# A convolution and maxout kernel on one core: x loads with three buffers, output stores moved to SyncE's queue, DMA transposes placed ahead of loads

## The chip, the cores and the metric

The kernel runs on one core of a Trainium2 chip. The time is device microseconds from launch to end; what is compared is the median over several runs. Before the change it is 467.4 us (five runs: 466.04, 466.86, 467.4, 467.55, 468.59).

## The reference

Input x has 8 sequences of 4160 tokens with 192 channels. First comes a causal convolution of 7 taps along the sequence, whose weights are a softmax per head (8 heads of 24 channels). Then every token goes through a maxout layer: three products with 192x768 weights, the largest of the three, and a product with a 768x192 weight.

```python
w = exp(weight - max) / (sum + 1e-9)                        # 8 heads x 7 taps
y[b, s, h, :] = sum_k w[h, k] * x_pad[b, s + k, h, :]        # 6 zero rows ahead of each sequence
h = np.maximum(np.maximum(y @ w1, y @ w2), y @ w3)           # 33280 x 768
out = h @ w_out                                              # 33280 x 192
```

## The kernel before

**Blocks.** The 33280 tokens are cut into 65 blocks of 512. Blocks 0 to 3 ("dense") take one road through the convolution, all later ones another. Blocks from 5 are convolved in pairs and from 17 (QUADS) in fours: one convolution serves four blocks.

**Stages of a later block.** `load_x(t)` (L129) brings 512 tokens of x into an fp32 buffer `xf` by two (sometimes three, once eight) DMAs on SyncE's queue, SP. There are seven such buffers (XBUF, L116), used in turn; `get_x` (L118) clears the unused rows of a buffer once, with a memset on GpSimd (POOL). `cast_x(t)` (L169) turns xf into fp16 by two POOL instructions, and frees the buffer. `conv` multiplies with a banded matrix on TensorE (L326), `evac` (L367) copies the sums out of PSUM to `ys`, `turn(t)` (L378) sends them through DMA transposes (L388, on SP) into `yp`, channels on partitions, and `double(t)` (L391) copies each half of `yp` to the other half of the partitions, by POOL, for blocks 4 and 5 by two DMAs on SP. `l1(t, j)` (L460 on) makes the first layer in six parts (L473: products lp and lq on the two halves of TensorE's rows; ScalarE and VectorE make the maximum, L480, L481). `st2(t, upto)` makes the second layer (L530); `total` adds its two halves into an output tile `o` (L538, L539), and `store` (L558 on) sends it away.

**Dense blocks.** Blocks 0 to 3 are cast by `cast_dense` (L189, block 2 and 3 wholly on POOL, L198), convolved by `conv_dense` (L345), and their halves are crossed between partitions, for block 3 by `cross_dma` (L363), two DMAs `yd<-yd` on SP (L365, L366).

**The order.** It is written out by hand. Each engine, and SP, does its instructions in the order in which the program names them. `op(fn)` puts a call behind the matmuls that are queued so far, `meet()` lets all queued work be placed. Ahead of the main loop (L617 to L634) stand the casts of `wo`, loads of blocks 6 to 10 among the rest, and `cast_dense(2)` and `(3)`. The loop over t (L653 on) makes, in turn t, the first layer of block t and the second of block t-1; `convs_at` (L643) says which later block is convolved in that turn (t is `late` where there is one); `casts` (L646) and `loads` (L649) say up to which block has been cast and loaded by turn t, about 8 and 10 blocks on:

```python
loads = {t: min(NB - 1, max(10, casts.get(t + 1, 0) + 1)) for t in range(3, NB)}
...
        if t > 3:
            for v in range(loads[t - 1] + 1, loads[t] + 1):
                load_x(v)
...
        op(lambda t=t: store(t - 2, 0, 4, (nc.gpsimd if t < NB - 1 else nc.sync,)))
...
                if second:
                    turn(u)
```

So in a turn the loads stand first on SP, and the transposes, four in a row for four blocks (in turn u - 3), behind them. Stores are issued from POOL (L569), each behind a wait for VectorE's last sum of that block (L539).

Of the kernel before, what the change touches and what calls it, by code (L numbers as in the profile page):

```python
# [28 lines left out]
def kernel(  # L29
# [12 lines left out]
    nc = tc.nc  # L42
# [27 lines left out]
    NB = len(blocks)  # L70
# [15 lines left out]
    NDENSE = 4  # L86
# [31 lines left out]
    def get_x(t):  # L118

        if not 0 <= t < NB or t in xin:  # L120
            return
        if t < XBUF:
            xbuf.append(const.tile([P, NR, D], FP32, name=f"xf_{t}"))
        xf = xbuf[t % XBUF]
        if NDENSE <= t < NDENSE + XBUF:
            nc.gpsimd.memset(xf[TOK:HALF, 0 if t < XBUF else NQ:NR, :], 0.0)  # L126
        xin[t] = [xf, 0, ()]

    def load_x(t, eng=nc.sync):  # L129
        if not 0 <= t < NB:  # L130
            return
        get_x(t)
        xf = xin[t][0]
        if t < NDENSE:
            todo = [(0, c[3], c[1] * SEQ + c[2], i) for i, c in enumerate(chunks_of[t])]
        else:
            todo = [(HALF * (i // NR) + (0 if s else LAP), KR if s else TOK,
                     b * SEQ + s - (LAP if s else 0), i % NR) for i, (b, s) in enumerate(rows_of(t))]
        parts = []
        i, n = 0, len(todo)  # L140
        row = [c[2] for c in todo]
        while i < n:
            k = i
            while k + 1 < n and todo[k + 1][:2] == todo[i][:2] and row[k + 1] - row[k] == row[i + 1] - row[i]:
                k += 1
            step = row[i + 1] - row[i] if k > i else 0
            p0, rlen, _, q0 = todo[i]
            q1 = todo[k][3] + 1
            src = bass.AP(tensor=x.tensor, offset=row[i] * D,
                          ap=[[D, rlen], [step * D, q1 - q0], [1, D]])  # L150
            eng.dma_start(out=xf[p0:p0 + rlen, q0:q1, :], in_=src)  # L151
            if parts and parts[-1][0] == rlen:
                parts[-1] = (rlen, parts[-1][1], q1)
            else:
                parts.append((rlen, q0, q1))
            i = k + 1
        xin[t] = [xf, todo[0][0], parts]
# [4 lines left out]
        pairs[t] = (t - u, u, 2 if t < QUADS else 4)  # L162

    def place(t):
        return pairs[t]

    x16s, slots = {}, {}

# [18 lines left out]
    xz[2], xz[3] = xz[0], xz[1]  # L187

    def cast_dense(t, copies):  # L189
        xf, _, parts = xin[t]  # L190
        for v, copy in enumerate(copies):
            if copy is None:
                continue
            for s in range(CYC // 32):
                cut = GRP * (32 * s // GRP + 1)
                a, b = (32 * s, cut) if v == 0 else (cut, 32 * s + 32)
                for (rl, q0, q1) in parts:
                    copy(  # L198
                        out=xz[t][v][0:rl, q0:q1, :].rearrange("p q (k c) -> p q k c", c=CYC)[:, :, :, a:b],
                        in_=xf[0:rl, q0:q1, :].rearrange("p q (k c) -> p q k c", c=CYC)[:, :, :, a:b])  # L200
# [174 lines left out]
                 "p u r (h c) -> p h (u r) c", c=GRP),  # L375
             in_=G[i][:].rearrange("p h (n c) -> p h n c", c=GRP))

    def turn(t):  # L378


        nu = place(t)[2]
        for v in range(0, nu, 2):
            n = min(nu, 2)
            yp = ypp.tile([P, 2, 2, n, NC, P], FP16, tag="yp", name=f"yp_{t + v}")
            for u in range(n):
                dense[t + v + u] = yp
            for i in range(2):
                nc.sync.dma_start_transpose(out=yp[:, 0, i, :, :, :].rearrange("p u k n -> p (u k) n"),  # L388
                                            in_=slots[t][:, i, v:v + n, :, :].rearrange("p u r d -> p (u r d)"))

    def double(t, by_dma=False):  # L391

        if not NDENSE <= t < NB:
            return
        yp = dense[t]
        copy = nc.sync.dma_start if by_dma else nc.gpsimd.tensor_copy
        for i in range(2):
            copy(out=yp[HALF * i:HALF * (i + 1), 1, :, :, :, :].rearrange("p i u k n -> p (i u k n)"),  # L398
                 in_=yp[HALF * (1 - i):HALF * (2 - i), 0, :, :, :, :].rearrange("p i u k n -> p (i u k n)"))
# [35 lines left out]
    def op(fn):  # L435
        ops.append((tuple(put), fn))
# [178 lines left out]
    l1(0, 4)  # L615
    meet()
    nc.gpsimd.tensor_copy(out=wo[:], in_=wos[:])  # L617
    for t in range(6, 9):
        load_x(t)
    l1(0, 5, WW)  # L620
    meet()
    make_m(0)
    make_m(1)
    cast_dense(2, (nc.gpsimd.tensor_copy, nc.gpsimd.tensor_copy))
    load_x(9)
    l1(1, 4)
    meet()
    st2(0, (5, 5))
    meet()
    conv_dense(2, (nc.scalar.copy, nc.vector.tensor_copy, nc.scalar.copy))  # L630
    cast_dense(3, (nc.gpsimd.tensor_copy, nc.gpsimd.tensor_copy))
    load_x(10)
    cast_x(4)
    cross(2)  # L634
    l1(1, 5)
# [10 lines left out]
    casts = {4: 9}  # L646
    for t in range(5, NB):
        casts[t] = min(NB - 1, casts[t - 1] + (2 if t in (6, 9, 12) else 1))
    loads = {t: min(NB - 1, max(10, casts.get(t + 1, 0) + 1)) for t in range(3, NB)}  # L649
    EVEN = [5, 10, 15, 20, 25, 30]  # L650
    ROOM = [5, 13, 17, 21, 26, 30]
    OWN, AHEAD = 3, 4
    for t in range(2, NB):  # L653
        u = convs_at.get(t, NB)
        late = t > 2 and u < NB
        if t in (3, 4):
            double(t + 1, True)
        if t > 3:
            for v in range(loads[t - 1] + 1, loads[t] + 1):
                load_x(v)  # L660
            for v in range(casts.get(t - 1, 8) + 1, casts[t] + 1):
                cast_x(v)
        l1(t, 0)
        if t == 2:
            meet()
            conv_dense(3, (nc.scalar.copy, nc.vector.tensor_copy, nc.scalar.copy))
            cross_dma(3)
            conv(u, PQ)
            evac(u, 0)
            evac(u, 1, nc.vector.tensor_copy)  # L670
            turn(4)
            cast_x(5)
            cast_x(6)
        elif t == 3:
            cast_x(7)
            cast_x(8)
        op(lambda t=t: store(t - 2, 0, 4, (nc.gpsimd if t < NB - 1 else nc.sync,)))
        cuts = ROOM if late else EVEN
        st2(t - 1, (cuts[0], cuts[0]))
        for j in range(1, NJ):  # L680
            l1(t, j)
            if late and j == 1:
                st2(t - 1, (cuts[0] + OWN + AHEAD, cuts[0] + OWN))
                meet()
                quad, second = u >= QUADS, u < QUADS or t == u - 3
                conv(u, WPWQ, range(4 * second, 4 * second + 4) if quad else range(NHEAD))
                for i in (0, 2):
                    evac(u, i)
                for i in (1, 3):
                    evac(u, i, nc.vector.tensor_copy)  # L690
                if second:
                    turn(u)
            st2(t - 1, (cuts[j], cuts[j]))
            if j == 1 and t > 4 and t + 2 in pairs and pairs[t + 2][1] % 2 == 0:
                double(t + 2)
            if t == NB - 1 and j == 3:
                op(lambda: store(NB - 2, 0, 2, (nc.sync,)))
        if t == NB - 1:
            op(lambda: store(NB - 2, 2, 4, (nc.sync,)))
# [31 lines left out]
```

## Time and profile before

| what | value |
|---|---|
| median of five runs | 467.4 us (466.04 to 468.59) |
| the profiled execution's own time | 473.36 us |
| its span | 471.6 us |
| TensorE (PE) busy | 452.9 us, 96% |
| VectorE (DVE), ScalarE (ACT), POOL busy | 76%, 68%, 53% |
| 16 DMA engines: SP's queue (q1) | 47.15 MB in 95631 packets, 51.1% |
| POOL's queue (q0) | 24.38 MB in 6960 packets, 15.0% |
| TensorE's instructions (q8) | 1.00 MB in 61 packets, 1.0% |
| stores issued from POOL, 384 KB each | 61, 751 ns of POOL each, 3.9 us to landing |

The profile is of one execution. Times in it run from the span's start. PE is TensorE, PEld its weight loads, SPq what SyncE's sequencer issues and waits for. A wait is written "engine what <- what it waited for: us in total, times, longest". "issue" is time in which an engine waited for nothing that the profile shows.

### The profile page before, as it was taken

The numbers are of one execution on the slowest core, as the hardware profiler recorded it, in microseconds if no ns is written. First come the engines' busy times: TensorE is split into PE (matmuls) and PEld (weight loads), VectorE is DVE, ScalarE is ACT, GpSimd is POOL, SyncE is SP. The second block draws the span as 40 slices with busy tenths as digits, with TensorE's granted clock in tenths as the row PEclk, the third lists the DMA queues.
The fourth block names the chain that finished last, engine by engine and source line by source line (L and its number), as shares of the span: only waits on it lengthen the run. The fifth ranks groups of instructions, "written<-read, shape, count | busy, mean of one in ns | idle before, by whom it ended". The sixth has DMA issues, their size and how long they took to land.

```text
span 471.6 us, 18658 instructions
## 1 busy us (share of the span) xinstructions
PE 452.9 (96%) x7783; PEld 416.7 (88%) x7783; DVE 359.2 (76%) x616; ACT 319.0 (68%) x609; POOL 249.8 (53%) x286
## 2 busy tenths in 40 slices
PE   7996989899999999999999989999999999999996
PEld 3574979899999999999899989999999999999996
DVE  6763766777878787787777878787878878787775
ACT  5753756666767777676677757676777767676664
POOL 5692365547655564556655553665555455534300
PEclk9898999999999999999999999999999999999999
DMA  8998799669674895749476793848568583215113
GB/s 193 209 201 152 138 193 186 161 141 200 169 183 149 154 183 142 223 98 187 144 178 166 144 210 96 194 133 175 153 181 188 120 215 112 93 69 114 59 69 101
DMA packets 102836, 72.83 MB, mean 154 GB/s; under 512 B 52064, under 2 KB 97647, under 8 KB 102751
## 3 DMA queue, kind: packets, MB, share of 16 engines
q1 hardware_dynamic: 95631, 47.15, 51.1%
q0 software_dynamic: 6960, 24.38, 15.0%
q8 instruction: 61, 1.00, 1.0%
q14 instruction: 24, 0.20, 0.2%
q10 hardware_dynamic: 160, 0.10, 0.1%
HBM read 33.28 MB, written 25.56 MB: 125 GB/s over the span
## 4 chain that ended last, share of the span: by engine, by line
PE 91%; DMA 4%; SPq 2%; issue 1%; POOL 1%; DVE 0%; ACT 0%; DVEq 0%
PE po L530 35%; PE lq L473 30%; PE lp L473 22%; PE G L326 4%; DMA wos<-in_moe_w_out_dram 3%; DMA yd<-yd 2%; SPq L211 1%; PE D L345 0%; POOL xz L198 0%; SPq L151 0%; POOL wo L617 0%; POOL xf L126 0%; PE pm L302 0%; PE pm L306 0%; ACT r L480 0%
## 5 line engine op out<-in xcount | busy, mean ns | idle before, releaser
L481 DVE TENSOR_TENSOR h<-r,lq 128x512 f16<-128x512 f16 x386 | 264.7, 686 | 96.7 <-ACT r L480 87.9
L530 PE MATMUL po<-wo,h 64*128 64x192 f16 x3120 | 336.9, 243 | 0.0
L480 ACT ACTIVATE r<-lp 128x512 f16<-128x512 f32 x386 | 230.5, 597 | 121.2 <-PE lp L473 102.2
L473 PE MATMUL lp<-yp,wd 64*128 64x512 f16 x1098 | 296.8, 377 | 0.0
L473 PE MATMUL lq<-yp,wd 64*128 64x512 f16 x1098 | 296.4, 377 | 0.0
L530 PEld LDWEIGHTS <-h 64*128 64x128 f16 x3120 | 247.2, 94 | 7.1 <-issue 4.0
L473 PEld LDWEIGHTS <-wd 64*128 64x128 f16 x2340 | 183.6, 95 | 21.0 <-DMA yd<-yd 3.4
L530 PE MATMUL po<-m,yp 64*128 64x192 f16 x732 | 143.8, 244 | 0.0
L569 POOL DMA_DIRECT2D out_dram<-o x63 | 47.3, 751 | 169.7 <-DVE o L539 132.8
L181 POOL CAST x<-xf 103x768 f16<-103x768 f32 x122 | 97.1, 828 | 19.5 <-PE G L326 9.8
L398 POOL COPY yp<-yp 64x1536 f16<-64x1536 f16 x58 | 84.8, 1463 | 5.3 <-DMA yp<-ys 2.5
L539 DVE TENSOR_TENSOR o<-a,po 128x384 f32<-128x384 f32 (+1 forms) x132 | 71.4, 542 | 0.6 <-ACT a L538 0.6
L530 PEld LDWEIGHTS <-yp 64*128 64x128 f16 x732 | 67.6, 94 | 0.4
L538 ACT COPY a<-po 128x384 f32<-128x384 f32 (+1 forms) x132 | 61.8, 469 | 2.1 <-PE po L530 1.9
L374 ACT CAST ys<-G 128x384 f16<-128x384 f32 x61 | 26.6, 481 | 15.5 <-PE G L326 15.2
L374 DVE CAST ys<-G 128x384 f16<-128x384 f32 x61 | 31.3, 550 | 4.4 <-PE G L326 4.4
L326 PE MATMUL G<-x,band 39*32 39x192 f16 (+2 forms) x1216 | 18.7, 231 | 5.6 <-issue 5.6
L473 PE MATMUL lq<-yd,wd 64*128 64x512 f16 x60 | 18.2, 407 | 3.6 <-DMA yd<-yd 3.0
L326 PEld LDWEIGHTS <-band 39*32 39x32 f16 x1216 | 11.4, 92 | 11.2 <-issue 11.1
L473 PE MATMUL lp<-yd,wd 64*128 64x512 f16 x60 | 18.1, 407 | 1.9 <-DMA yd<-yd 1.3
L345 PEld LDWEIGHTS <-xz 112*32 112x32 f16 x240 | 5.0, 107 | 4.2 <-POOL xz L198 2.6
L345 PE MATMUL D<-band,xz 112*32 112x103 f16 (+1 forms) x240 | 6.5, 229 | 1.7 <-POOL xz L198 1.0
(52 smaller groups left out, 78.3 us busy)
## 6 DMA issues: line engine op xcount, KB each, us to landing
xf<-in_x_dram SPq DMA_DIRECT2D x113, 234.0 KB
out_dram<-o POOLq DMA_DIRECT2D x61, 384.0 KB, 3.9
xf<-in_x_dram SPq DMA_DIRECT2D x7, 204.8 KB
xf<-in_x_dram SPq DMA_DIRECT2D x3, 420.0 KB
ws<-in_moe_w_dram SPq DMA_DIRECT2D x6, 192.0 KB
yp<-ys SPq DMA_TRANSPOSE x62
w3s<-in_moe_w_dram SPq DMA_DIRECT2D x3, 192.0 KB
wos<-in_moe_w_out_dram SPq DMA_DIRECT2D x1, 576.0 KB
```

What stands on the lines that cost most here:

```text
L181: nc.gpsimd.tensor_copy(out=x16s[t0][0:K, :, :, u, r, :].rearrange("p h j c -> p j h c"), in_=xf[0:K, 4 * r:4 * r + 4, :].rearrange("p j ( ...
L326: nc.tensor.matmul(G[2 * (k // per) + i][TOK * j:TOK * (j + 1), k % per, :], lhsT=band[row, h, HALF * i + LAP:HALF * i + KR], rhs=x16s[t0] ...
L345: nc.tensor.matmul(ps[32 * g:32 * g + 32, lo:hi], lhsT=xz[t][v][0:rlen, q, 32 * s:32 * s + 32], rhs=band[0:rlen, h, cc:cc + hi - lo], star ...
L374: copy(out=slots[t][:, i % 2, :, :, GRP * h0:GRP * (h0 + per)].rearrange("p u r (h c) -> p h (u r) c", c=GRP), in_=G[i][:].rearrange("p h ...
L398: copy(out=yp[HALF * i:HALF * (i + 1), 1, :, :, :, :].rearrange("p i u k n -> p (i u k n)"), in_=yp[HALF * (1 - i):HALF * (2 - i), 0, :, : ...
L473: nc.tensor.matmul(ps[i][:], lhsT=wd[HALF * i:HALF * (i + 1), c, P * j:P * (j + 1)], rhs=y_all(t, i, c), start=(c == 0), stop=(c == NC - 1))
L480: nc.scalar.activation(out=r[:], in_=ps[0][:], func=AF.Relu)
L481: nc.vector.tensor_max(out=hs[t][:, j, :], in0=r[:], in1=ps[1][:])
L530: nc.tensor.matmul(ps[b0, i][:, s % 2, :], lhsT=a, rhs=b, start=first, stop=last)
L538: nc.scalar.copy(out=a[:, ss, :], in_=ps[s0, 0][:, ss, :])
L539: nc.vector.tensor_add(out=outs[t][:, s0:s + 1, :], in0=a[:, ss, :], in1=ps[s0, 1][:, ss, :])
L569: qs[0].dma_start(out=bass.AP(tensor=out.tensor, offset=r * D, ap=[[D, n], [step * D, s1 - s0], [1, D]]), in_=ob[p0:p0 + n, s0:s1, :])
```

## The change

- From block 11 on, loads go round three buffers (those of blocks 4, 5 and 6) in place of seven, so load v waits for the cast of block v - 3. Blocks 4 to 10 have the seven buffers once.
- All stores are issued by SP, in the turn where POOL issued them, and the loads of the turn stand behind the store: at once in turns without a convolution, and behind the convolution's copies and its transposes in `late` turns.
- `turn` is given which pairs of a four it transposes: the first pair in turn u - 3 as before, the second in turn u - 2, between the store and the loads.
- Ahead of the loop only blocks 6 and 7 are loaded. Block 8 is loaded behind the transposes of block 4, block 9 behind `double(4)`, block 10 in turn 3 behind the transposes of block 5. Their memsets on POOL move with them.
- `place` and `cast_dense` change only in bookkeeping (an assertion keeps a buffer from being given out twice).

The instructions of TensorE, VectorE and ScalarE are the same in kind, number and order. SP's list grows from 128 to 190, POOL's shrinks from 199 to 137.

```diff
-        xf = xbuf[t % XBUF]
+        xf = xbuf[t % XBUF if t < NDENSE + XBUF else NDENSE + (t - NDENSE - XBUF) % 3]
...
-    def turn(t):
+    def turn(t, vs=(0,)):
...
-        for v in range(0, nu, 2):
+        for v in vs:
...
-    for t in range(6, 9):
+    for t in (6, 7):
         load_x(t)
...
     cast_dense(2, (nc.gpsimd.tensor_copy, nc.gpsimd.tensor_copy))
-    load_x(9)
...
     cast_dense(3, (nc.gpsimd.tensor_copy, nc.gpsimd.tensor_copy))
-    load_x(10)
     cast_x(4)
...
-    loads = {t: min(NB - 1, max(10, casts.get(t + 1, 0) + 1)) for t in range(3, NB)}
+    loads = {t: min(NB - 1, casts.get(t + 1, 0) + 1) for t in range(4, NB)}
+    loads.update({2: 9, 3: 10})
+
+    def load_on(t):
+        for v in range(loads[t - 1] + 1, loads[t] + 1):
+            load_x(v)
...
+        if t == 3:
+            load_x(9)
         if t > 3:
-            for v in range(loads[t - 1] + 1, loads[t] + 1):
-                load_x(v)
...
             turn(4)
+            load_x(8)
             cast_x(5)
...
-        op(lambda t=t: store(t - 2, 0, 4, (nc.gpsimd if t < NB - 1 else nc.sync,)))
+        if t > 3 and not late:
+            op(lambda t=t: (store(t - 2, 0, 4, (nc.sync,)),
+                            turn(t + 2, (2,)) if place(t + 2)[1:] == (0, 4) else None, load_on(t)))
+        else:
+            op(lambda t=t: store(t - 2, 0, 4, (nc.sync,)))
...
                 if second:
                     turn(u)
+                load_on(t)
```

## The prediction

> **What bounds the kernel now.** I read the page's busy time and slices first, then the chain that ended last, then the waits of TensorE and of SP, and last the timelines around each place where TensorE stood still.
>
> ```profile
> PE 452.9 (96%) x7783; PEld 416.7 (88%) x7783; DVE 359.2 (76%) x616; ACT 319.0 (68%) x609; POOL 249.8 (53%) x286
> ...
> PE   7996989899999999999999989999999999999996
> ...
> PE 91%; DMA 4%; SPq 2%; issue 1%; POOL 1%; DVE 0%; ACT 0%; DVEq 0%
> ```
>
> TensorE is the bound: 91% of the chain is its matmuls. Nothing in the change takes a matmul away, so only its idle time can be won. The chain's "DMA 4%", "issue 1%" and "POOL 1%" are where to look. TensorE's own waits, over the whole span:
>
> ```profile
> PE G L326 <- issue: 5.6, 5, 1.9
> PE lq L473 <- DMA yd<-yd: 3.0, 1, 3.0
> PE lp L473 <- DMA yd<-yd: 1.3, 1, 1.3
> ...
> PE D L345 <- POOL xz L198: 1.0, 2, 0.6
> ```
>
> Three kinds. First, block 3's first layer waits 3.0 + 1.3 us for the crossing DMAs. SP's timeline says why they are late (start, duration, what):
>
> ```profile
> 19.89 13.28 SPq L151 DMA_DIRECT2D xf<-in_x_dram  x12
> 33.65 1.67 SPq L365 DMA_DIRECT2D yd<-yd  x1
> 35.42 0.56 SPq L366 DMA_DIRECT2D yd<-yd  x1
> ```
>
> Loads up to block 10 stand ahead of them. The crossing's data is ready at 32.1 and 32.5 (ends of the evictions L354, L352), it is issued at 33.65 and 35.42, and TensorE goes on at 41.09 and 42.82. Second, five stops inside the convolution with no releaser, which the chain dates:
>
> ```profile
> 67.52 1.92 issue
> 84.63 1.38 issue
> 99.64 0.29 issue
> 226.73 0.64 issue
> 280.76 1.34 issue
> ```
>
> The packets of TensorE's instruction queue explain these (q8: 61 packets of 16 KB for 15,566 matmuls and weight loads, some 255 each). In quiet stretches they start about 7 us apart. The one ahead of the stop at 226.73 started at 224.7, 14.2 us after its forerunner at 210.5; that ahead of 280.76 at 279.3, 14.7 us after 264.6. Each stop ends 1.3 to 1.6 us after such a packet has ended. Gaps of some 12 us (242.0 to 254.1, 296.8 to 309.1) cost no stop. And the late ones fall into bursts of loads:
>
> ```profile
> 208.05 6.11 SPq L388 DMA_TRANSPOSE yp<-ys  x4
> 214.26 5.78 SPq L151 DMA_DIRECT2D xf<-in_x_dram  x9
> ```
>
> With seven buffers a load finds its buffer free, so what holds SP is only the transposes, and behind them four blocks' loads go out at once (9 DMAs, 2.1 MB, DMA share 0.94 from 216 to 226). Third, the half clock after stops (columns: window, sum, PE, PEld, DVE, ACT, POOL busy, PEclk, DMA share, GB/s):
>
> ```profile
> 43.00:50.00 7.00, 7.00 (x140) 5.57 (x138) 3.79 (x7) 3.78 (x8) 1.60 (x2) 0.82 0.46 84
> 60.00:70.00 10.00, 8.08 (x177) 7.45 (x174) 6.58 (x12) 5.56 (x11) 7.51 (x8) 0.97 0.94 195
> 70.00:80.00 10.00, 10.00 (x132) 9.34 (x130) 6.51 (x12) 6.20 (x12) 4.26 (x5) 0.86 1.05 192
> 127.00:450.00 323.00, 321.02 (x5383) 304.40 (x5381) 257.33 (x433) 228.88 (x434) 175.36 (x187) 1.00 0.63 151
> ```
>
> PEclk 0.82 over 7 us and 0.97, 0.86 over 20 us are one stretch of 3.41 us each at half clock, at 42.06 and 69.36.
>
> **What each stop costs, from block lengths.** The trace's first L473 product of each block gives lengths. An undisturbed block takes 6.36 us, with a pair's convolution 7.15 (block 4), with half a four's 6.92. Block 3 takes 13.33: 6.2 over 7.15. Blocks 6, 8 and 10 take 10.75, 8.65 and 7.56: 3.6, 1.5 and 0.4 over. Blocks 29 and 37, at 224.0 and 278.0, take 7.81 and 8.52: 0.9 and 1.6 over 6.92. So the crossing costs 6.2 us and the instruction stops 8.0 us in this execution.
>
> **The change, part by part.**
>
> *Loads 8, 9, 10 behind the crossing* take 3 x 468 KB off SP's queue ahead of it; which is the 7.4 us in which the packets of those three blocks passed (30.2 to 37.6); the queue is then empty from about 30.2. The crossing is issued when its data is ready, 32.0 to 33.2, and lands some 2 us later (a 192 KB store alone on SP near the end: issued 462.90, landed 464.84), about 35.3. TensorE wants it at 37.7. Cover 2.4 us; the 6.2 us go. If the cover failed by d, d comes back, and 1.8 us of half clock with it once the stop is long. What is late next is block 8's x, behind the transposes, landing about 40 where its cast (36.43 now) is wanted by the convolution at 47, and block 4's doubling: two DMAs behind load 8 and the first store, landing near 42 for block 4's start at 44.4. Block 5's doubling stands behind load 10, about 49 to 50 for 51.5. These covers are 1.5 to 2.5 us.
>
> *The memset of block 8's buffer* leaves POOL's list ahead of cast_dense(2):
>
> ```profile
> 21.80 2.40 POOL L126 MEMSET xf<- 32x1536 f32 x3
> 24.27 1.64 POOL L198 CAST xz<-xf 112x240 f16<-112x240 f32 x6
> ```
>
> The convolution L345 of block 2 waits for these casts. One 32x576 memset is 0.57: 0.57 us gained. The two of blocks 9 and 10 have no wait behind them that TensorE sees: nothing.
>
> *Stores to SP*: 62 issues of about 0.4 to 0.6 us on SP in place of 751 ns on POOL. POOL waits 132.8 us at them for VectorE now; its casts become earlier, which TensorE doesn't notice in steady work. On SP each waits for the same L539 sum, which ends about 1 us into the turn, and behind it stand the turn's transposes and loads. Per four blocks SP issues 4 stores (2.4 us), 4 transposes (6.1), 8 loads (5.2): 13.7 us of 26.58. In the transfers a store now goes by 768-byte packets of 36 ns (the stores on SP at the end) and not by 4608-byte ones of about 155: 512 x 36 / 16 = 1.15 us in place of 85 x 155 / 16 = 0.82; in a burst, at the loads' 70 ns, 2.2. No store is followed by anything on the path.
>
> *Loads one by one.* Load v waits for the cast of v - 3, which stands a turn or more ahead on POOL. Its two DMAs go out at 1 us into a turn, or 7 us where transposes stand ahead, and take 624 packets at 215 a us (the burst's rate) = 2.9 us. The cast is two turns on, 13 us, and the convolution later still: cover at least 3 us to the cast, some 8 more to TensorE. DMA work per four blocks: loads 11.6, stores 4 x 1.4 (the 370 packets a us of the end), transposes 4 x 1.0 (768 packets at 750 a us) = 21.2 of 26.58 us, with no burst over two DMAs' worth plus a store and two transposes, about 6 us against 12 now. The fetch was late by 7 us in a burst of 12; by about half that in the new one. A stop comes at some 5 us of lateness (12 us apart cost nothing, 14.2 cost 0.9). So the 8.0 us go, all or nearly.
>
> *Second pair of transposes a turn later*: needed by POOL's doubling in turn u, the result in turn u + 2: two turns of cover. Nothing.
>
> [...]
>
> **The sum.** Against the profiled execution: 471.6 - 6.2 - 0.6 - 8.0 = 456.8 span, 458.6 with the 1.8 us around it. The runs lie 6 us below the profiled time. Without its instruction stops it would be 473.4 - 8.0 = 465.4, just under the fastest run (466.04), so I take it that the runs carry the crossing but only some 1 to 3 us of instruction stops, 2.0 in the median, which also fits their spread of 2.5 us. Then 467.4 - 6.8 - 2 = 458.6; 0.6 is added for a small new wait at block 4 or 5: 459.2.
>
> **Rivals.**
> 1. *Larger*: the runs carry all 8.0 us of stops, and the 6 us between profile and runs are something else: 467.4 - 14.8 = 452.6. For it: nothing shows what those 6 us are. Against: 465.4 falls so close to the runs.
> [...]
> 3. *No effect*: the crossing is as late as now, since its DMAs are slow themselves (they share the engines with the transposes and the store at 36 to 41). Then 466 to 467.4. Against: their packets follow block 10's at once.
> 4. *Slower*: everything in one in-order queue of SP, with the engines near full. Where all packets go at the 200 a us of the burst's slowest stretch (219 to 223), a load takes 3.1 us, a store 2.6, and with transposes at twice their time (one at 49 to 52 shows that) four blocks need 12.5 + 10.2 + 8.2 = 30.9 us against 26.58. Loads then fall behind, and once their 11 us of cover are eaten TensorE runs at the queue's pace. With 12 fours it decides against the change from 27.3 us a four (0.7 x 12 = 8.2, the whole gain); at 27.9 the time is 459.2 + 16 = 475. Against: those rates belong to a full queue, and the share is 0.63 in steady work.
>
> **How the numbers follow.** Likeliest 0.62 (456 to 461.5), larger 0.12 (452 to 456), partial 0.13 (461.5 to 465), no effect 0.05, slower 0.08. A measurement tells 0.3% (1.4 us) from no change. Faster 0.87, same 0.05, slower 0.08. The range 454 to 464.5 leaves out about a third of "larger", the end of "partial", and the last two: just under 0.2.
>
> **What would show it.** Right: no wait of TensorE for yd<-yd, the crossing issued before 33.5; full clock from 20 us on; q8 packets 7 us apart with no 14 us gap, no "issue" rows of over 0.3 us in the chain; SP's loads in twos; block 3 of about 7.1 us. Wrong: a wait of L473 for `yp`, of POOL's casts for xf that reaches L326, SP waiting for VectorE at L570 with loads late behind it, or DMA share near 1 in steady work.

## The result and the profile after

The changed kernel takes 461.65 us (median of 41 runs, 459.7 to 465.2); the kernel before, run beside it, 467.76 (76 runs, 460.46 to 475.38). The ratio is 0.9927, with a 95% interval of 0.9911 to 0.9942: faster by 0.7%. The medians of all runs stand at 0.987, 6.1 us apart; the ratio is nearer to 1 because it is taken over the runs within 1.5% of each kernel's fastest, which leaves out 42 of the 76 of before. So the change is faster, by less than the 8.2 us of the forecast: by 3.4 us (0.73% of 467.8) by the ratio, by 6.1 by the medians.

The profiled execution of the changed kernel is one of 461.65 us, span 459.8, and so a run like the median. That of before (473.36) lies in the upper part of before's scatter. Between the two profiles there are 11.8 us of span, more than between the medians. The page of after, its busy time, slices and chain:

```profile
PE 451.1 (98%) x7783; PEld 415.4 (90%) x7783; DVE 359.6 (78%) x616; ACT 319.0 (69%) x609; POOL 203.7 (44%) x223
...
PE   8969999999999999999999999999999999999997
...
PE 92%; DMA 2%; POOL 2%; issue 1%; SPq 1%; DVE 1%; ACT 0%; POOLq 0%; DVEq 0%
```

TensorE's busy time is as before (452.9, 451.1); from the fourth slice to the last but one there is nothing but nines. TensorE's waits in the span, the largest ahead:

```profile
PE G L327 <- issue: 3.2, 1, 3.2
PE idle L236 <- DVE idle L231: 1.2, 1, 1.2
...
```

Behind these two are only two of 0.2 us. The wait of block 3 for `yd<-yd` (3.0 + 1.3) is gone, and of the five stops by "issue" one is left, which before did not have: 3.21 us at 29.30, inside the convolution of block 4. TensorE's timeline there:

```profile
29.07 0.24 PE L327 MATMUL G<-x,band 39*32 39x48 f16 x14
32.52 0.55 PE L327 MATMUL G<-x,band 39*32 39x48 f16 x50 [3.21 <-issue]
```

Fourteen products, then nothing, then the other fifty. And half clock follows (window, sum, busy PE, PEld, DVE, ACT, POOL, granted clock, DMA share, GB/s):

```profile
33.27:36.69 3.42, 3.42 (x30) 1.98 (x27) 1.15 (x2) 0.95 (x2) 1.77 (x3) 0.50 0.17 36
...
118.00:440.00 322.00, 322.00 (x5405) 305.31 (x5402) 258.11 (x436) 229.81 (x435) 138.27 (x137) 1.00 0.71 153
```

The last row is the steady work: TensorE busy in 322.00 of 322 us, full clock, DMA share 0.71 (before: 321.02 of 323, and 0.63). SP's timeline shows the crossing issued as soon as its data is there, and in steady work the loads in twos behind stores:

```profile
29.78 0.64 SPq L366 DMA_DIRECT2D yd<-yd  x1
30.52 1.00 SPq L367 DMA_DIRECT2D yd<-yd  x1
...
183.93 0.42 SPq L570 DMA_DIRECT2D out_dram<-o  x1
184.44 1.17 SPq L152 DMA_DIRECT2D xf<-in_x_dram  x2
190.29 0.41 SPq L570 DMA_DIRECT2D out_dram<-o  x1
190.79 0.99 SPq L152 DMA_DIRECT2D xf<-in_x_dram  x2
```

What sets this pace is SP's own wait:

```profile
SPq L570 <- DVE o L540: 178.9, 60, 6.6
```

60 stores, each held until VectorE has made the sum: SP stands still for 178.9 us, and the loads behind it with it.

**Where the time went, block by block.** As in the prediction, a block's length is the distance between the first L474 (before: L473) products of two blocks, in the two profiled executions. The blocks that are not listed take 6.36, 6.92 or 7.15 us in both, within 0.02 (blocks 0 and 1 are the start):

| block | before | after | change |
|---|---|---|---|
| start of block 2 | 29.62 | 26.72 | -2.9 |
| 2 | 8.09 | 13.68 | +5.6 |
| 3 | 13.33 | 7.14 | -6.2 |
| 6 | 10.75 | 7.28 | -3.5 |
| 8 | 8.65 | 7.15 | -1.5 |
| 10 | 7.55 | 7.28 | -0.3 |
| 29 | 7.81 | 6.92 | -0.9 |
| 37 | 8.51 | 6.92 | -1.6 |

The rows come to -11.3. The crossing's 6.2 and the stops' 7.8 went, nearly as the prediction had them (6.2 and 8.0). But 5.6 came back one block earlier: a new stop of 3.2 with half clock behind it. The 2.9 ahead of block 2 holds the 0.57 of the memset; I put the rest down to the load of `wo` (not shown by a run of its own), whose place on SP the change doesn't touch: its cast on POOL begins at 18.22 after, and before at 20.60, behind a wait for that load:

```profile
20.60 1.14 POOL L617 CAST wo<-wos 128x1152 f16<-128x1152 f32 x1 [1.42 <-DMA wos<-in_moe_w_out_dram]
```

In the profiles of all runs below it begins between 16.9 and 19.2, also where the opening is that of before (18.18 in e8). So the profiled execution of before was late here, it seems by chance.

What this table can't tell is which of these differences the *median* runs have. The experiments are for that.

### The profile page after: what moved, and what is told of

Its sections match the earlier page's. It is cut to its first block, busy times and chain, and to the rows that moved or that the text cites. A ratio compares the mean times of both kernels' runs of the same rounds, so it can differ in the third digit from the quotient of the medians.

```text
span 459.8 us, 18658 instructions
## 1 busy us (share of the span) xinstructions
PE 451.1 (98%) x7783; PEld 415.4 (90%) x7783; DVE 359.6 (78%) x616; ACT 319.0 (69%) x609; POOL 203.7 (44%) x223
## 3 DMA queue, kind: packets, MB, share of 16 engines
q1 hardware_dynamic: 128383, 71.54, 71.4%
## 4 chain that ended last, share of the span: by engine, by line
PE 92%; DMA 2%; POOL 2%; issue 1%; SPq 1%; DVE 1%; ACT 0%; POOLq 0%; DVEq 0%
PE po L531 36%; PE lq L474 31%; PE lp L474 22%; PE G L327 3%; DMA w3s<-in_moe_w_dram 2%; SPq L212 1%; DVE yd L362 0%; POOL wd L279 0%; POOL w3s L283 0%; SPq L152 0%; POOL xz L199 0%; PE D L346 0%; POOL wo L618 0%; DVE o L540 0%; POOL xf L126 0%
## 5 line engine op out<-in xcount | busy, mean ns | idle before, releaser
L474 PE MATMUL lp<-yp,wd 64*128 64x512 f16 x1098 | 295.6, 376 | 0.0
L474 PE MATMUL lq<-yp,wd 64*128 64x512 f16 x1098 | 295.5, 376 | 0.0
L474 PEld LDWEIGHTS <-wd 64*128 64x128 f16 x2340 | 182.0, 94 | 15.0 <-issue 2.3
L327 PEld LDWEIGHTS <-band 39*32 39x32 f16 x1216 | 11.3, 91 | 8.5 <-issue 8.0
L474 PE MATMUL lq<-yd,wd 64*128 64x512 f16 x60 | 17.9, 400 | 0.2 <-DVE h L482 0.2
L474 PE MATMUL lp<-yd,wd 64*128 64x512 f16 x60 | 17.9, 401 | 0.0
L531 PE MATMUL po<-m,yd 64*128 64x192 f16 x48 | 7.2, 251 | 0.0
L236 PE MATMUL idle<-idle 128*128 128x512 f16 x13 | 5.8, 588 | 1.2 <-DVE idle L231 1.2
```

What stands on the lines that cost most here:

```text
L236: nc.tensor.matmul(ps[:], lhsT=idle[:, 0:P], rhs=idle[:], start=True, stop=True)
L327: nc.tensor.matmul(G[2 * (k // per) + i][TOK * j:TOK * (j + 1), k % per, :], lhsT=band[row, h, HALF * i + LAP:HALF * i + KR], rhs=x16s[t0] ...
L474: nc.tensor.matmul(ps[i][:], lhsT=wd[HALF * i:HALF * (i + 1), c, P * j:P * (j + 1)], rhs=y_all(t, i, c), start=(c == 0), stop=(c == NC - 1))
L531: nc.tensor.matmul(ps[b0, i][:, s % 2, :], lhsT=a, rhs=b, start=first, stop=last)
```

## The experiments

Each is an edit of the changed kernel, unless it says "of before". Medians are given with the lowest and highest run; the median of before beside it, in the same set of runs, was 467.8 (e0 to e3), 467.19 (e4, e5, e7, e8), 469.17 (e9 to e12), 468.18 (e13 to e15) and 467.24 (e16 to e18).

### The two halves of the change, each alone

**e0_change**: the change itself, beside the next three.

> The changed kernel once more, for its opening. Theory A (the instruction fetch is late in the opening, behind the loads of blocks 4 to 7, because the convolutions there use up instructions twice as fast): this profile again has a stop of 2 to 4 us with no releaser ahead of the convolution of block 4, with half clock behind it, and the time is 461 to 462.5 us. Theory B (that stop was chance in one execution): no such stop in this profile, and the lost 2.5 us lie elsewhere, spread over later blocks.

461.63 us (459.3 to 465.07), 0.9876 [0.9827, 0.9925]. A second profile, and again the one stop of block 2, 3.4 us, and nothing behind it.

**e1_early_alone**: of before, with nothing but loads 8, 9 and 10 moved behind the crossing.

```diff
-    for t in range(6, 9):
+    for t in (6, 7):
         load_x(t)
...
-    load_x(9)
...
-    load_x(10)
...
+        if t == 3:
+            load_x(9)
...
             turn(4)
+            load_x(8)
...
+                if t == 3:
+                    load_x(10)
```

> The kernel before with nothing but the loads of blocks 8, 9 and 10 moved behind the crossing of block 3 (stores on POOL, seven buffers, all transposes as before). Theory A: the wait for the crossing (6.2 us with its half clock) goes, the opening's stop of about 5 us comes in its place, the stops in the bursts of loads stay at some 2 us: 463 to 466 us. Theory B: the opening's stop is chance, 459.5 to 461.5 us.

467.95 us (462.75 to 472.15, 22 runs) against 467.8: ratio 0.9984 [0.9958, 1.001]. The part that was to bring 6.8 us brings nothing that can be measured, less than either theory's range had. Its profile, of its lowest run (462.75), has no wait for `yd<-yd`, so the edit does what it says; but it has four stops by issue in the convolution, and a late doubling. What the median executions have it can't tell:

```profile
PE G L326 <- issue: 3.7, 4, 1.8
...
PE lq L473 <- DMA yp<-yp: 1.1, 1, 1.1
```

**e2_late_alone**: the change with loads 8, 9, 10 back ahead of the loop, so that only the later parts (stores on SP, three buffers, transposes split) are left.

```diff
-    for t in (6, 7):
+    for t in range(6, 9):
         load_x(t)
...
+    load_x(9)
...
+    load_x(10)
...
-        if t == 3:
-            load_x(9)
...
-            load_x(8)
```

> The changed kernel with the loads of blocks 8, 9 and 10 back ahead of the loop as before; three buffers, stores on SP and split transposes stay. Both theories: block 3 waits 4 to 6 us for the crossing as before. No stop over 0.3 us from block 6 on. If the stops in the bursts weigh 2 us in the median, 465.5 us; if they weigh the 8 us that the first profile showed, 460 us.

462.4 us (460.63 to 463.89), 0.988 [0.984, 0.992]: nearly the whole gain, and the early part on top of it is worth 462.4 - 461.63 = 0.8 us, with ranges that overlap. The profile says how the crossing can be late and cost nothing. SP, and TensorE's waits:

```profile
32.34 0.70 SPq L366 DMA_DIRECT2D yd<-yd  x1
33.13 0.55 SPq L367 DMA_DIRECT2D yd<-yd  x1
```

```profile
PE G L327 <- issue: 2.5, 1, 2.5
...
```

The crossing is again issued at 32.3 and 33.1 behind the loads, and lands at 39.7 and 40.0. No wait for it: TensorE stopped for 2.5 us in block 2 and then ran at half clock, so block 3 begins at 41.81 only. In this opening the loads hold up two things, the crossing (issued at 32.3, landed at 39.7) and the fetch of TensorE's instructions (a stop of 2.5 us), and whichever is later hides the other.

### Which of the later parts it is

**e5_seven_buffers**: the change, with seven buffers again.

```diff
-        xf = xbuf[t % XBUF if t < NDENSE + XBUF else NDENSE + (t - NDENSE - XBUF) % 3]
+        xf = xbuf[t % XBUF]
```

> The changed kernel with seven buffers throughout; the loads still stand behind a store, which waits for VectorE. Theory C: the stores pace the loads, 461 to 462.5 us. Rival (the three buffers do it): bursts come back, 464 to 467 us with stops in the convolutions.

460.9 us (458.71 to 463.07), 0.9881 [0.9829, 0.9933]. The three buffers add nothing that these runs can tell from zero.

**e4_pool_stores**: the change, with the stores back on POOL.

```diff
-            op(lambda t=t: (store(t - 2, 0, 4, (nc.sync,)),
+            op(lambda t=t: (store(t - 2, 0, 4, (nc.gpsimd if t < NB - 1 else nc.sync,)),
...
-            op(lambda t=t: store(t - 2, 0, 4, (nc.sync,)))
+            op(lambda t=t: store(t - 2, 0, 4, (nc.gpsimd if t < NB - 1 else nc.sync,)))
```

> The changed kernel with its stores back on POOL; three buffers, split transposes and the order of the loads stay. Theory C (what is won is the pacing of the loads, so that a fetch of TensorE's instructions finds at most one block's loads in front of it; either the wait for a buffer or the wait for a store does it): as the changed kernel, 461 to 462.5 us, no stop over 0.3 us from block 5 on. Rival (the stores' move itself is the gain, because a store in a queue of its own competes with the fetch): 464 to 467 us.

468.03 us (464.43 to 475.52, 22 runs), 1.0034 [1.0003, 1.0065]: the whole gain is lost, and theory C, in which the wait for a buffer paces the loads as well, is wrong. SP's timeline shows that three buffers do not let loads loose one by one:

```profile
179.64 2.55 SPq L389 DMA_TRANSPOSE yp<-ys  x2
182.28 5.07 SPq L152 DMA_DIRECT2D xf<-in_x_dram  x6
```

POOL's casts are so far ahead that the buffers are free; the transposes hold SP, and then three blocks' loads go out together. The chain dates the stops of steady work, in an execution of 468.48 us, near the median:

```profile
143.19 1.16 issue
197.78 0.38 issue
251.39 0.59 issue
305.41 0.88 issue
```

Blocks 17, 25, 33 and 41 take 8.14, 7.69, 7.67 and 8.14 us in place of 6.92, blocks 5, 6 and 8 2.3 us more than in the change.

**e7_pool_seven**: both edits together (of the two store lines one is shown).

```diff
-        xf = xbuf[t % XBUF if t < NDENSE + XBUF else NDENSE + (t - NDENSE - XBUF) % 3]
+        xf = xbuf[t % XBUF]
...
-            op(lambda t=t: store(t - 2, 0, 4, (nc.sync,)))
+            op(lambda t=t: store(t - 2, 0, 4, (nc.gpsimd if t < NB - 1 else nc.sync,)))
```

> The changed kernel with stores on POOL and seven buffers, so that neither holds a load; split transposes and the early order stay. Theory C: SP runs ahead again between its transposes, bursts of two to three blocks' loads, some of the stops come back: 463.5 to 466.5 us, q8 packets over 12 us apart in places. Rival (the pacing isn't it, the transposes' split or their place ahead of the loads is): 461 to 462.5 us.

467.48 us (465.14 to 474.51, 22 runs), 1.0049 [1.0021, 1.0077]: as e4. What is left of the change here, the early loads and the split transposes, gains nothing together.

**e8_before_three**: of before, with three buffers only. Loads stand ahead of the casts there, so in turns in which two blocks are cast a load overwrites x before its cast, and a part of the output is computed from other rows of x; the work is the same.

```diff
-        xf = xbuf[t % XBUF]
+        xf = xbuf[t % XBUF if t < NDENSE + XBUF else NDENSE + (t - NDENSE - XBUF) % 3]
```

> The kernel before with nothing changed but three buffers from block 11 on. Theory C: the waits for buffers alone pace the loads from about block 7, so the stops there go; those at blocks 5 to 6 and the crossing stay: 463 to 465 us. Rival (pacing by buffers alone holds up SP, and the transposes queued behind the held load come late): 467 us or more, with waits for yp.

471.04 us (469.62 to 475.87), 1.0114 [1.0055, 1.0172]: slower. Here the buffers do hold loads back, and that is what costs. SP's wait, and TensorE's:

```profile
SPq L151 <- POOL x L181: 62.4, 32, 7.5
```

```profile
PE lq L473 <- DMA yp<-yp: 2.0, 1, 2.0
...
PE lp L473 <- POOL yp L398: 1.2, 1, 1.2
```

A held load holds the transposes behind it, and through the doubling (L398) blocks 12 and 13, which take 8.46 and 9.72 us in place of 7.15 and 6.92. The change's order, transposes ahead of loads, is meant to avoid that; it was not tried by itself.

The opening of e8 is that of before, for the three buffers act from block 11 on. It returns under "The opening".

### What the stores do on SP: pace, or queue

Two ways are open. On SP a store waits for VectorE, and so paces the loads behind it. Or the store's packets, in a queue of their own when POOL issues them (q0, 24.38 MB in before), hold up the fetch, and no longer do in SP's queue (q1, 71.54 MB in after, with no q0). e11 tells how far pace alone goes, e12 how far the queue alone goes, e13 takes e12's queue away, and e14 moves e12's bursts to another place.

The table has, from the q8 packets of each profile, how late a fetch of TensorE's instructions starts. The stops tell which instruction is the first that a fetch brings: in before those behind the stops at 67.52 and 226.73 are 5364 matmuls and weight loads and 21 fetches apart, 255.4 to a fetch. Counted from there, fetches in quiet stretches start 240 to 260 instructions ahead (fetches 45 to 48 of before 251, 253, 256 and 254, fetch 53 261), one whole fetch, so about when TensorE begins the block of instructions before; "late" is counted from 260 ahead. Fetches 18, 25, 32 and 39 are those that have the whole convolution of blocks 17, 25, 33 and 41 in that block of instructions (eight blocks of tokens use exactly seven fetches: the stops in blocks 29 and 37 of before are 1788 instructions apart, seven times 255.4); 28 and 35, which the stops in blocks 29 and 37 waited for, have only 8 to 13 of its 32 products there.

| kernel | stores | loads | late, us: 18, 25, 32, 39 | late, us: 28, 35 | median, us |
|---|---|---|---|---|---|
| before | POOL | four blocks | 3.2, 2.4, 4.0, 4.3 | **6.2, 6.9** | 467.76 |
| change | SP | one block | 3.0, 3.9, 2.5, 2.6 | under 2, 3.4 | 461.65 |
| e4 | POOL | three blocks | **5.7, 5.5, 5.6, 5.7** | under 2, 5.2 | 468.03 |
| e11 | 3/4 POOL | one block | 3.1, 2.7, 2.1, under 2 | 2.1, 2.5 | 460.02 |
| e12 | SP | four blocks | 2.2, 3.7, 2.7, 3.2 | 4.2, 5.6 | 460.38 |
| e13 | POOL | four blocks | 4.0, 2.7, 3.7, 4.8 | under 2, 4.3 | 469.76 |
| e14 | SP | three blocks | **5.4**, 4.2, **5.8, 5.4** | under 2, 2.4 | 465.62 |

Bold are those behind which TensorE stopped for over 0.3 us in the profile. A stop is the lateness less the time to spare: 6.2 with 0.64 and 6.9 with 1.34 us of stop give 5.6 us to spare at 28 and 35; 5.5 to 5.7 with 0.38 to 1.16 (e4) give 4.5 to 5.1 at the other four.

**e11_quarter_on_sp**: three quarters of each store from POOL, one quarter from SP where the store stood.

```diff
+    def parted(t):
+        if t < NB - 1:
+            store(t - 2, 0, 3, (nc.gpsimd,))
+            store(t - 2, 3, 4, (nc.sync,))
+        else:
+            store(t - 2, 0, 4, (nc.sync,))
...
-            op(lambda t=t: store(t - 2, 0, 4, (nc.sync,)))
+            op(lambda t=t: parted(t))
```

> The changed kernel with three quarters of each store back on POOL's queue and one quarter left on SP, in the same place and with the same wait for VectorE. SP's loads stay paced by that wait, while most of the store's bytes go by POOL's queue. Pacing theory (the store matters because SP waits in it, so the loads come one block at a time): 461 to 463 us, no stop over 0.3 us from block 11 on. Queue theory (the store matters because it no longer goes by a queue of its own beside the loads and the fetch): 465 to 468 us, stops at blocks 17, 25, 33 and 41 as with all stores on POOL.

460.02 us (459.09 to 462.13), 0.9853 [0.9806, 0.99]. SP's timeline has a block's two loads behind each part of a store, and POOL's queue 18.29 MB (packets, MB, share of 16 engines):

```profile
181.95 0.38 SPq L570 DMA_DIRECT2D out_dram<-o  x1
182.42 0.83 SPq L152 DMA_DIRECT2D xf<-in_x_dram  x2
```

```profile
q0 software_dynamic: 4976, 18.29, 11.6%
```

The pace is enough, or nearly: with three quarters of the store bytes still on POOL's queue, the gain is whole. (A quarter of the bytes did move; a wait on SP without any store there was not tried.)

**e12_loads_by_fours**: the opposite. Stores on SP, seven buffers, and four blocks' loads together in turns 14, 18, 22 and so on.

```diff
-        xf = xbuf[t % XBUF if t < NDENSE + XBUF else NDENSE + (t - NDENSE - XBUF) % 3]
+        xf = xbuf[t % XBUF]
...
+    each = dict(loads)
+    for t in range(QUADS - 3, NB):
+        loads[t] = each[min(NB - 1, t - (t - QUADS + 3) % 4 + 3)]
```

> The changed kernel, stores on SP, with seven buffers and, from turn 14, the loads of four blocks let go together behind the first pair's transposes (turns 14, 18, 22 and so on) and none in the other turns. Pacing theory: bursts of eight loads make the fetch late by 6 to 7 us again; stops at the convolutions of some or all fours, 464 to 470 us. Queue theory: as with seven buffers and paced loads, 460 to 462 us.

460.38 us (459.75 to 463.04), 0.9857 [0.9811, 0.9904]; no wait of TensorE from 80 to 460 us. The bursts are as large as in before (there nine DMAs in 5.78 us):

```profile
199.24 6.64 SPq L152 DMA_DIRECT2D xf<-in_x_dram  x8
```

Yet there is no stop. So the pace is not needed either.

**e13_fours_pool_stores**: e12 with the stores on POOL (the diff of e4 on top).

> The kernel with loads by fours once more, but with the stores on POOL: the bursts stand where they stood, only the stores' queue differs. Queue matters (a store in a queue of its own beside a burst makes the fetch later by another 1 to 2 us): 464 to 468 us with stops in the convolutions. Place matters (a burst costs only where it meets the fetch that the convolution of blocks 17, 25, 33 ... needs, which has the least time to spare, and here it meets others): 460 to 462 us.

469.76 us (463.98 to 472.93, 12 runs), 1.0026 [0.9969, 1.0084]: 9.4 us over e12's median, and 1.7% by the two ratios. With e4 (1.0034 against e0's 0.9876) and e7 (1.0049 against e5's 0.9881) these are three pairs that differ in the stores' queue alone, and all three lie 1.6 to 1.7% apart, some 7.5 us (by the medians 6.4, 6.6 and 9.4), whatever the buffers and the order of the loads.

But the pair doesn't show that it is under the bursts that the queue decides. The profile of e13 is of an execution of 465.55 us, 5.8 over e12's. Blocks 2, 5 and 6 are 2.7, 1.2 and 1.5 us longer in it than in e12's, and the bursts begin only in turn 14; from there on blocks 14, 22 and 46 are longer by 1.3 together. The stops by issue in its chain from 29 us on are 3.27 at 29.27, 1.37 at 65.11, 0.25 at 174.19 and 0.48 at 334.15, against e12's 1.67 at 29.74 alone. And its fetches are hardly later than e12's: from fetch 14 to 57 they are late by 2.0 us in the mean against 1.5, the latest by 5.1 against 5.6. Block 2's share may be chance, for in three profiles of the change itself block 2 takes 13.68, 12.96 and 10.28 us. What the executions near e13's median have is open.

**e14_loads_by_threes**: e12 with three blocks' loads together in turns 15, 19, 23 and so on, behind the second pair's transposes.

```diff
+    each = dict(loads)
+    for t in range(QUADS - 2, NB):
+        loads[t] = each[min(NB - 1, t + (2, 1, 0, 0)[(t - QUADS + 2) % 4])]
```

> The changed kernel, stores on SP, with seven buffers and the loads of three blocks let go together behind the second pair's transposes (turns 15, 19, 23 and so on), which is the burst that SP made by itself when the stores were on POOL and stops came at blocks 17, 25, 33 and 41. Place matters: the stops at these blocks are back, 463 to 467 us. Queue matters: no stops, 460 to 462 us.

465.62 us (460.87 to 470.35, 20 runs), 0.9967 [0.9928, 1.0007]. A smaller burst than e12's, also with the stores on SP, and most of the gain is gone. TensorE's waits from 80 to 460 us:

```profile
PE po L531 <- issue: 1.8, 3, 0.8
...
```

The three are in blocks 17, 33 and 41, even in this execution of 460.87 us, its lowest. The burst now meets the fetches that have the whole convolution ahead of them, and with it the least to spare (4.5 to 5.1 us by the table, against 5.6).

### The opening

The stop of 3.2 us in block 2 is the largest thing left. In after, the fetch it waits for starts at 29.67, 5.2 us late, while the queue passes the loads of blocks 4 to 7.

The same stop stands in e8, whose opening is that of before (nothing waits for `yd<-yd` in it, and block 3 takes 7.14 us):

```profile
29.35 0.24 PE L326 MATMUL G<-x,band 39*32 39x48 f16 x14
33.26 0.55 PE L326 MATMUL G<-x,band 39*32 39x48 f16 x50 [3.67 <-issue]
```

There, as in after, `wo` was in time. In the profile of before `wo` was late and block 2 began 2.1 us later than in e8; the fetch was due later (27.3 against 25.3) and started sooner (28.2 against 30.2), so it cost no stop, and the crossing's wait came to light. So the wait that the forecast was built on may be one of that execution; a second one of the same opening has the stop in its place.

The runs that follow move the loads of blocks 6 and 7.

**e3_six_seven_later**: load 6 behind the crossing, 7 in place of 8, 8 behind the doubling of block 4.

```diff
-    for t in (6, 7):
-        load_x(t)
...
+            load_x(8)
...
+            load_x(6)
...
-            load_x(8)
+            load_x(7)
```

> The changed kernel with the loads of blocks 6 and 7 moved too: 6 behind the crossing, 7 in the place of 8, 8 behind the doubling of block 4. The queue then runs empty near 25 us. Theory A: the fetch ahead of the convolution of block 4 is in time, the stop and its half clock go, 456.5 to 458 us. Rival (the fetch is late for another reason than the loads in front of it): the stop stays, 461 to 462.5 us. If the doubling of block 4 or the cast of block 6 comes late instead, a wait of 1 to 2 us in block 3 or 4 shows it.

465.56 us (461.47 to 469.67, 22 runs), 0.9996 [0.9969, 1.0023]. The stop is gone, block 2 takes 8.09, but block 4's doubling and the casts are late now (TensorE's waits, the first two):

```profile
PE lp L474 <- DMA yp<-yp: 3.5, 1, 3.5
PE G L327 <- POOL x L182: 2.5, 2, 2.1
...
```

**e9_seven_only_later**: load 6 stays, 7 in place of 8, 8 behind the doubling of block 4.

```diff
-    for t in (6, 7):
-        load_x(t)
+    load_x(6)
...
+            load_x(8)
...
-            load_x(8)
+            load_x(7)
```

> For the opening: the changed kernel with the load of block 7 alone moved to the place of 8, and 8 behind the doubling of block 4. The queue in front of the fetch at 24 us is 468 KB, some 2.3 us, shorter. If the stop ahead of block 4's convolution comes from that queue, it falls from 3.3 us to about 1, and the time by 2 to 4 us to 458 to 460 us, unless block 7's or 8's cast comes late for the convolution in block 4: then 461 to 463 us with a wait for POOL's cast there.

462.65 us (461.25 to 463.51), 0.9896 [0.985, 0.9941]. Block 2 takes 8.50, but block 4 takes 13.01, with waits of 2.4 us for POOL's cast and 1.8 for the doubling.

**e10_six_seven_behind_casts**, and once more **e18_casts_again**: loads 6 and 7 stay ahead of the loop, behind the casts of blocks 2 and 3.

```diff
-    for t in (6, 7):
-        load_x(t)
...
+    load_x(6)
...
+    load_x(7)
```

> For the opening: the changed kernel with the loads of blocks 6 and 7, and their memsets, moved behind the casts of blocks 2 and 3, so that they are issued some 2 to 4 us later but still ahead of the crossing. The fetch that is asked for at 24 us then finds only block 5's rest and block 6 in front: stop 1 to 2 us in place of 3.3, and 1.4 us of memset off block 2's casts (the part that TensorE waits for, about 0.5): 458.5 to 460.5 us. If the stop does not shrink, the queue of loads is not what holds that fetch: 461 to 462 us.

> The opening with the loads of blocks 6 and 7 behind the casts, once more beside the changed kernel: 1 to 2.5 us below it if the gain of the first run is real, equal to it if that was the chip.

459.12 us (457.23 to 463.11), 0.9833 [0.9777, 0.9889], and 460.11 (459.12 to 461.63), 0.9851 [0.9807, 0.9896]. The stop is 1.1 and 0.3 us; the doubling of block 4 comes 1.2 and 1.9 us late in its place. The second is 0.7 us below the change beside it (e17), with ranges that overlap: a gain isn't shown.

**e15_both**: e10 and e11 together (their two diffs).

> The opening with the loads of blocks 6 and 7 behind the casts (459.1 alone, against 461.6) together with three quarters of each store on POOL's queue and a quarter on SP (460.0 alone). If both gains are real and independent 457.5 us; if the second is chance, 459 us.

461.82 us (457.59 to 465.26, 17 runs), 0.9907 [0.9873, 0.994]: not better than either, and above both values that were expected. No stop by issue is left in the loop, but `PE lp L474` waits 1.8 us for the doubling.

**e16_ten_behind_doubling**: e10, with load 10 behind the doubling of block 5. **e17_change_again**: the change beside it.

```diff
-    loads.update({2: 9, 3: 10})
+    loads.update({2: 10, 3: 10})
...
-        if t == 3:
-            load_x(9)
+        if t in (3, 4):
+            load_x(t + 6)
```

> The opening with the loads of blocks 6 and 7 behind the casts, and now also the load of block 10 behind the doubling of block 5, not ahead of it. The wait of block 5's first layer for yp (1.2 to 1.8 us in the last profiles) goes: 1 to 2.5 us below the version without it, measured beside it, so 457.5 to 459.5 us. If the wait was covered by the half clock or comes back at block 6 or 7: no difference.

> The changed kernel, as the measure beside the two opening versions on this chip: 460.5 to 462 us, with the stop of 2 to 4 us ahead of the convolution of block 4.

459.41 us (455.71 to 460.27), 0.9807 [0.9751, 0.9863], and for the change 460.82 (459.86 to 463.05), 0.987 [0.9824, 0.9916]. In e16's profile no wait of TensorE is over 1.2 us. Its median lies 1.4 us below the change's, but the intervals overlap.

## Why the prediction was wrong

**Right.** The direction; that the stops are late fetches of TensorE's instructions behind bursts of loads; that loads in twos end them; the crossing issued before 33.5, no wait for `yd<-yd`, block 3 of about 7.1 (7.14); no wait of steady work for the loads, so not the slower case. The lateness of the fetches was to fall by about half: from fetch 14 on the latest is 3.9 us late in after, 6.9 in before, and no two in after start over 11.3 us apart. That the second pair of transposes costs nothing wasn't tried by itself; in after nothing waits for it.

**The term that failed: 6.8 us for the crossing and the memset.** The sum was 467.4 - 6.8 - 2.0 + 0.6. e1, which is the first term alone, measured nothing (467.95 beside 467.8, at most 2 us by its interval), and on top of the other parts 0.8 (e2 against e0). In the profile of before the crossing did cost 6.2, and in after it is gone; the step that failed is that the runs all carry this wait and that nothing takes its place. The three loads that were moved were not what held the fetch in block 2: those of blocks 4 to 7 are, and they stayed ahead of it. With them ahead, a stop of 1.8 to 3.4 us stands in block 2 in all three profiles of the change, one block ahead of the wait that was removed, and e2 shows that such a stop hides the crossing. It stands in e8 too, at 3.67 us, with the opening of before: there TensorE doesn't wait for the crossing, and its 6.2 us are not there to be won. "Full clock from 20 us on" and "no issue rows of over 0.3" were wrong at this one place.

**The other term was too small: 2.0 us for the stops.** Alone, the later parts measured 467.8 - 462.4 = 5.4 us. The 2.0 came from the argument that the runs lie 6 us below the profile because they carry the crossing but few of the stops. That was read out of one profile and five runs. Over 76 runs before scatters by 15 us (460.46 to 475.38), and its profile lies in the upper part of that; the changed kernel scatters by 5.5. Five runs within 2.5 us had made the profile look like an exception to be explained, and the forecast kept the wrong part of it: the crossing as common, the stops as rare. The two errors have opposite signs, and it is luck that the forecast of 459.2 lies within 2.5 us of the median: with the measured terms in place, 467.8 - 5.4 - 0.8 = 461.6.

**The credit went to the wrong edit.** "Stores to SP" was costed at nothing, and "loads one by one" to three buffers. The runs say that the stores do it (e4, e7, e13: without them on SP the gain is gone; e5: three buffers add nothing). By their wait for VectorE they are what lets loads loose one by one, and a quarter of each store is enough for that (e11). A burst with the stores on SP cost nothing either where it met fetches with 5.6 us to spare (e12, 460.38 us), though it did where they had 4.5 to 5.1 (e14, 465.62).

**What the fetches met.** In the traces the latest fetches lie in bursts of loads: in before they started up to 6.9 us late, with some 1440 packets of loads going by between the moment the latest was due and its start, some 90 on each of the 16 engines if they are spread evenly (an estimate). By what way so many come ahead of one fetch no run here shows. On the clock, after's half clock (3.41 us) followed a stop of 3.21 us, before's of 69.36 one of 1.92; the last section has what the traces show of it. A slip without effect on the sum: packets of 4608 bytes took 178 ns in the median (before's q0), not about 155.

**What stays open.** How often executions of before carry the crossing's wait, and how often the stop in block 2: one profile has the first, one of the same opening (e8) the second. By what way stores on POOL cost some 7.5 us: in e4 and e7 late fetches in blocks 17 (e4), 25, 33 and 41 are a part of it, in e13 hardly. And whether the stores on SP would do it alone: the kernel before with nothing else changed was not run.

## What to carry to other kernels

In this kernel a DMA issue that waited was a pacer for all that stood behind it on SP: the stores (178.9 us of waits in after) for the loads, the held loads of e8 (62.4 us) for the transposes. Before moving such an issue, ask what it will hold back, and before crediting a pace to buffers, look in the trace whether anything ever waits for one. When a stretch is bound by a full queue, list everything that the queue holds up, here a crossing (6.2 us) and a fetch of instructions (5.6 us in block 2); taking one late item out may only uncover the next. And don't build a sum on the difference between one profile and a median of five runs; a few repeats of the part by itself size it better, and a second profile shows whether the first is typical.

## What the runs showed of the hardware

How late a fetch of TensorE's instructions could start without a stop differed with what TensorE had to do meanwhile. A fetch (a q8 packet, 61 for 15,566 matmuls and weight loads) brings some 255 instructions and starts, in quiet stretches, 240 to 260 ahead of the first of them, so about when TensorE begins the 260 before. In before and after TensorE takes these 260 in 7.0 us where a whole convolution of four blocks is among them (fetches 18, 25, 32 and 39; its 32 products, with their weight loads, take 0.45 us), and, stops left out, in 7.9 to 8.0 where only 8 to 13 of these products are (fetches 28 and 35). A fetch could start 4.5 to 5.1 us late without a stop in the first case (e4), and some 5.6 in the second (before), both worked out as under the table. In this kernel a place in the program meets the same place in a fetch every eight blocks (1788 instructions, seven fetches), and so a burst three blocks long cost more in one turn (e14, 465.62 us) than one of four blocks a turn earlier (e12, 460.38).

Whether half clock follows a stop can't be read from the stop's length alone: 1.92 us at 67.52 (before) was followed by 3.41 us at half clock, and 1.80 at 88.59 (e1) by products of 0.43 us in place of 0.22; 2.68 at 28.52 (e11), 1.76 at 29.04 (e17) and 1.67 at 29.74 (e12) had no such stretch behind them (granted clock of the whole execution 0.998, 1.000 and 0.999; one stretch of 3.41 us, as in after, makes it 0.996). In the traces of before and after the stretches at half clock begin whole multiples of 3.41 us apart: at 11.34, 42.06, 69.36 and 472.14 in before, 9, 8 and 118 times that, and at 33.27 and 459.94 in after, 125 times. Cut into lengths of 3.41 us from these starts, the two traces have, from 20 us on and up to the last products, TensorE idle for 3.03 and 1.84 us (before, from 38.64 and 65.95) and 2.66 us (after, from 29.86) in the lengths just ahead of half clock, and for 1.38 us at the most in all others (before, from 83.02). Before's stop of 1.92 us lies but for 0.08 in one such length, e11's longer one across the edge of two (columns as above; two rows of before, then two of e11):

```profile
65.95:69.36 3.41, 1.57 (x69) 1.25 (x64) 1.91 (x4) 1.11 (x3) 3.41 (x5) 1.00 0.91 176
69.36:72.77 3.41, 3.33 (x37) 2.81 (x38) 1.23 (x3) 1.44 (x3) 1.76 (x3) 0.50 1.32 226
...
26.45:29.86 3.41, 1.94 (x80) 1.21 (x77) 2.95 (x6) 2.18 (x4) 2.73 (x4) 1.00 0.73 154
29.86:33.27 3.41, 2.07 (x78) 1.67 (x79) 0.56 (x1) 0.80 (x2) 3.22 (x5) 1.00 0.47 150
```

Idle are 3.41 - 1.57 = 1.84 us in before's, 1.47 and 1.34 in e11's two. So in these traces it was in part luck of its place whether a stop cost half clock; what sets the clock they don't show.
